# The first gated block's transposition, by squares and DRAM in place of TensorE, inside the output projection

## The chip, the cores and the metric

The kernel runs on one core of a Trainium2 chip. The metric is the time of one execution on the device in microseconds (us), the median of several runs; lower is better. One execution was also recorded by the hardware profiler. TensorE does the matmuls, VectorE (DVE in the profile) and ScalarE (ACT) the elementwise work and the copies out of the accumulators, GpSimd (POOL) small work and some transfers, and SyncE (SP) issues most transfers. ScalarE can issue transfers too.

## The reference

Two layers, each an attention block and a gated block, with a residual and a layer norm ahead of each. There are 2048 tokens of width 448, 16 heads of width 28, and a hidden width of 1792.

```python
def _A_ref(x, wqkv, wo):                      # attention
    qkv = (x @ wqkv).reshape(B, S, 3, H, Dh).transpose(2, 0, 3, 1, 4)
    q, k, v = qkv[0], qkv[1], qkv[2]
    p = _softmax(jnp.einsum("bhqd,bhkd->bhqk", q, k) * (Dh ** -0.5))
    o = jnp.einsum("bhqk,bhkd->bhqd", p, v)
    return o.transpose(0, 2, 1, 3).reshape(B, S, D) @ wo
def _B_ref(x, w_gate, w_up, w_down):          # gated block
    h = _sigmoid(x @ w_gate) * (x @ w_up)
    return h @ w_down
x = A_x
for layer in range(2):                        # written out in the reference
    x = x + _A_ref(_layernorm(x), A_wqkv, A_wo)
    x = x + _B_ref(_layernorm(x), B_w_gate, B_w_up, B_w_down)
```

## The kernel before

The residual `x` stays in SBUF as 16 tiles of 128 tokens by 448 features. Four tiles make a block of 512 tokens (`TB` = 4, `NB` = 4). Operands of matmuls are pairs of float16 numbers, a high part and a low part, so one exact product costs several matmuls.

The order of instructions on every engine is that in which the program emits them. There is no scheduler (`manual_schedule`); semaphores are set between engines where tiles depend on each other. An instruction that waits holds everything behind it on its engine, and a transfer that waits holds everything behind it on its queue.

A layer has four stages: `project` (queries, keys, values), `attend`, `out_project` and `gated`. This case is about the seam between the last two.

`out_project` multiplies the 16 token tiles with the output weights, 11 matmuls of 448 columns for each tile: nine for the feature groups 0 to 2 (lines 517 to 519), two for the tail (lines 514 and 515), which holds the last head. Six tiles are done early without their tails (`early` = 6), since the last head's rows come late by transfers; then the six tails, then the other ten tiles. After each tile VectorE adds the result onto `x` (`add`, line 1199).

The gated block works on a `Block` of 512 tokens: layer norm (`stats`, `scale`), transposition to features by tokens, and a list of seven steps, `half_steps`, which builds the operands of a product scheme by halves: `r11`, `t1`, `t2`, `t3` make the four parts of `wide`, and `r21`, `t4`, `r22` make the three parts of `short`. Every step makes one high part by a copy on ScalarE (`divide`), one low part by a subtraction on VectorE, and mostly a difference on VectorE (`subtract`). The last three also copy a part from 64 lower partitions to the upper ones on ScalarE (`double`, line 376).

There are two ways to transpose. TensorE does it with an identity matrix, 16 transposes a block (`turn`, line 443), and ScalarE copies the result out of the accumulators (`turn_raw`, line 455). Or VectorE transposes squares of 32 by 32 (`squares`, line 295), the result is written to DRAM (`store`, line 307), and read back with rows and columns of squares in place (`gather`, line 315). With the second way the tokens lie in an order of squares, and a step that reads the gathered tile does so in two operations of half the size, where the first way takes one (the `cut`, `subtract` and `divide` of `half_steps`). The later blocks of `gated` use the second way; the first block, made inside `out_project`, uses the first.

`gated` emits, for each block and each pair of weight columns `p`, the products of `gate_and_up` on TensorE, in this order: `first(0)`, `first(1)`, `apart(0)`, `second(0)`, `second(1)` and so on. `first(0)` and `second(0)` are written to the same accumulator bank (`chain[0]`); between them ScalarE copies the bank out (line 1319). The products need `wide` for the first seven and `short` after that. Weights come in parts: `gu(p)` for gate and up, `dn` for down. `out_project` issues the loads of `gu(1)`, one `dn` and `gu(2)` on SyncE's queue at its start, and `gated` issues more at its own.

Of the kernel before, what the change touches and what calls it, by code (L numbers as in the profile page):

```python
# [16 lines left out]
ALU = mybir.AluOpType  # L17
AX = mybir.AxisListType

P = 128  # L20
S = 2048
D = 448
# [5 lines left out]
TB = NT // NB  # L28
W = TB * P
NF = F // P  # L30
NQ = D // 32
# [74 lines left out]
def interleaved_layers(ctx: ExitStack, tc: tile.TileContext, x_in, wqkv, wo, w_gate, w_up,  # L106
                       w_down, out):
    nc = tc.nc
# [6 lines left out]
    big = Slots(spool, "s", N_SLOTS)  # L115
# [5 lines left out]
    def new_banks():  # L121

        if banks["stack"] is not None:
            banks["stack"].close()
        uid[0] += 1
        banks["stack"] = ExitStack()
        banks["pool"] = banks["stack"].enter_context(
            tc.tile_pool(name=f"psum{uid[0]}", bufs=1, space=bass.MemoryType.PSUM,
                         reuse_waits="tile"))

    def psum(tag, name, shape):
        uid[0] += 1
        return banks["pool"].tile(shape, F32, name=f"{name}_{uid[0]}", tag=tag, bufs=1)
# [4 lines left out]
    def bank(i, name):  # L138
        return psum(f"bank{i}", name, [P, 512])
# [105 lines left out]
    class Block:  # L245
# [10 lines left out]
        def __init__(self, b, halves=False):  # L256
            self.b = b
            self.halves = halves
            self.turned = False

        def norm(self, js=range(TB)):
            b = self.b
# [77 lines left out]
        def half_steps(self):  # L340
            def cut(k, t):

                if self.turned:
                    return self.raw[:, k:k + 2, t * P:(t + 2) * P]
                return self.raw[:, k:k + 2, :].rearrange(
                    "p k (i t c) -> p k t i c", i=4, t=TB)[:, :, t:t + 2]

            def ordered(v):
                return v.rearrange("p k (t i c) -> p k t i c", t=2, i=4)

            def subtract(name, a, b):
                t = qrt.get(name, [P, 2, W // 2])
                if self.turned:
                    nc.vector.tensor_tensor(t, a, b, op=ALU.subtract)
                    return t
                a, b = [v if len(v.shape) == 5 else ordered(v) for v in (a, b)]
                for k in range(2):
                    nc.vector.tensor_tensor(ordered(t)[:, k], a[:, k], b[:, k],
                                            op=ALU.subtract)
                return t  # L360

            def divide(to, v):

                hi, lo = to[:, 0], to[:, 1]
                if len(v.shape) == 5:
                    for k in range(2):
                        nc.scalar.copy(ordered(hi)[:, k], v[:, k])
                        nc.vector.tensor_tensor(ordered(lo)[:, k], v[:, k], ordered(hi)[:, k],
                                                op=ALU.subtract)
                else:  # L370
                    nc.scalar.copy(hi, v)
                    nc.vector.tensor_tensor(lo, v, hi, op=ALU.subtract)

            def double(to):

                nc.scalar.copy(to[64:P, 0, 1], to[0:64, 0, 1])

            def r11():
                self.wide = big.get("xwide", [P, 4, 2, 2, W // 2], F16)
                self.short = big.get("xshort", [P, 3, 2, 2, W // 2], F16)  # L380
                self.t1 = subtract("t1", cut(0, 2), cut(0, 0))
                divide(self.wide[:, 0], cut(0, 0))

            def t1():
                self.t2 = subtract("t2", cut(2, 2), self.t1)
                divide(self.wide[:, 1], self.t1)
                qrt.put(self.t1)

            def t2():
                self.t3 = subtract("t3", cut(2, 2), cut(0, 2))  # L390
                divide(self.wide[:, 2], self.t2)

            def t3():
                self.t4 = subtract("t4", cut(2, 0), self.t2)
                nc.gpsimd.memset(self.t4[64:P, 1, :], 0.0)
                divide(self.wide[:, 3], self.t3)
                qrt.put(self.t2, self.t3)

            def r21():
                divide(self.short[:, 0], cut(2, 0))  # L400
                double(self.short[:, 0])

            def t4():
                divide(self.short[:, 1], self.t4)
                double(self.short[:, 1])
                qrt.put(self.t4)

            def r22():
                divide(self.short[:, 2], cut(2, 2))
                double(self.short[:, 2])  # L410
                big.put(self.raw)

            return [r11, t1, t2, t3, r21, t4, r22]

        def ready(self, *kts):
            if kts[0] == 0:
                self.parts()
            for kt in kts:
                self.part(kt)


        def begin(self):
            uid[0] += 1
            self.mv = cpool.tile([P, TB, 2], F32, name=f"mv_{uid[0]}", tag="mv", bufs=2)
            self.rs = cpool.tile([P, TB], F32, name=f"rs_{uid[0]}", tag="rs", bufs=2)
            self.xn = big.get("xn", [P, TB, D])
# [13 lines left out]
        def turn(self, j):  # L440
            for kt in self.pt:
                c = slice(kt * P, min((kt + 1) * P, D))
                nc.tensor.transpose(self.pt[kt][0:c.stop - c.start, j * P:(j + 1) * P],
                                    self.xn[:, j, c], ident)

        def turn_raw(self):
            self.turned = True
            self.turn_banks(4, range(4))
            self.raw = big.get("xraw", [P, 4, W])
            nc.gpsimd.memset(self.raw[64:P, 3, :], 0.0)  # L450
            for j in range(TB):
                self.turn(j)
            for kt, pt in self.pt.items():
                n = P if kt < 3 else 64
                nc.scalar.copy(self.raw[0:n, kt, :], pt[0:n])
            big.put(self.xn)

        def turned_high(self):
            for kt, pt in self.pt.items():
# [50 lines left out]
    def by_tokens(pm, hi, lo, tail, w, kts=range(4)):  # L510

        for kt in kts:
            if kt == 3:
                nc.tensor.matmul(pm, tail, w[:, 0, 3, :], start=False, stop=False)  # L514
                nc.tensor.matmul(pm, tail, w[:, 1, 3, :], start=False, stop=True)  # L515
                continue
            nc.tensor.matmul(pm, hi(kt), w[:, 0, kt, :], start=(kt == 0), stop=False)  # L517
            nc.tensor.matmul(pm, hi(kt), w[:, 1, kt, :], start=False, stop=False)  # L518
            nc.tensor.matmul(pm, lo(kt), w[:, 0, kt, :], start=False, stop=False)  # L519
# [88 lines left out]
    def run_fill(fill, n=1):  # L608
        for _ in range(n):
            if fill:  # L610
                fill.popleft()()
# [574 lines left out]
    def out_project(outs, gate):  # L1186
        new_banks()
        nc.scalar.activation(warm, warm, AF.Sigmoid)
        nc.scalar.reg_load(gate_scale, back.bitcast(I32)[0:1, 3:4])
        first = Block(0, True)  # L1190
        steps = deque([first.turn_raw] + first.half_steps())
        early = 6

        def products(pm, t, kts):
            by_tokens(pm, outs.hi(t), outs.lo(t), outs.tail(t) if 3 in kts else None, gate.out,
                      kts)

        def add(pm, t):
            nc.vector.scalar_tensor_tensor(x[:, t, :], pm, back[:, 1:2], x[:, t, :],
                                           op0=ALU.mult, op1=ALU.add)  # L1200

        gate.load_gu(1)
        gate.load_dn()
        gate.load_gu(2)
        pms = [bank(t, "op")[:, 0:D] for t in range(early)]
        for t in range(early):
            products(pms[t], t, range(3))
        first.begin()
        for t in range(early):
            products(pms[t], t, [3])  # L1210
            add(pms[t], t)
            if t < TB:
                first.stats(t)
            if t >= TB:
                first.scale(t - TB)
        for j in range(early - TB, TB):
            first.scale(j)
        for t in range(early, NT):
            pm = bank(t if t < 8 else t % 4, "op")[:, 0:D]
            products(pm, t, range(4))  # L1220
            add(pm, t)
            if t >= 9:
                run_fill(steps, 2 if t == 9 else 1)
        big.put(*outs.kt, gate.out)
        run_fill(steps, 9)
        return first
# [181 lines left out]
    first = Block(0)  # L1408
# [29 lines left out]
    for layer in range(LAYERS):  # L1438
        values, heads, last_values = project(layer, wq, first)
        gate = WeightsGated()  # L1440
        outs = attend(layer, values, heads, last_values, gate, wq.keep)
        mlp_first = out_project(outs, gate)
        wq = WeightsQKV()

        def before_next(f, wq=wq):
            if f == 6:
                wq.load()

        first = gated(layer, mlp_first, gate, before_next)
# [28 lines left out]
```

## Time and profile before

| | |
|---|---|
| time, median of 3 runs | 1940.18 us (1938.45 to 1941.05) |
| the profiled execution's own time | 1939.73 us |
| its span | 1937.9 us |
| granted TensorE clock, mean | 0.997 |
| TensorE busy | 1919.4 us, 99% of the span |
| VectorE busy | 1234.5 us, 64% |
| ScalarE busy | 1316.6 us, 68% |

A row of the timeline has the start in the span, the duration, the engine, the line, the operation with its output and inputs, the shapes and the count of instructions merged in it. In square brackets stand the idle time of the engine ahead of it and what ended that. The matmuls' durations overlap; the distance of two starts is what one costs. A row of the windows gives the busy time of each engine in a stretch, the granted TensorE clock as a share of full speed, the DMA engines' busy share and GB/s. A row of DMA issues has the size of each.

### The profile page before, as it was taken

The numbers are of one execution on the slowest core, as the hardware profiler recorded it, in microseconds if no ns is written. First come the engines' busy times: TensorE is split into PE (matmuls) and PEld (weight loads), VectorE is DVE, ScalarE is ACT, GpSimd is POOL, SyncE is SP. The second block draws the span as 40 slices with busy tenths as digits, with TensorE's granted clock in tenths as the row PEclk, the third lists the DMA queues.
The fourth block names the chain that finished last, engine by engine and source line by source line (L and its number), as shares of the span: only waits on it lengthen the run. The fifth ranks groups of instructions, "written<-read, shape, count | busy, mean of one in ns | idle before, by whom it ended". The sixth has DMA issues, their size and how long they took to land. (4 is left out here: it accounts for less than half of the span.)

```text
span 1937.9 us, 53581 instructions
## 1 busy us (share of the span) xinstructions
PE 1919.4 (99%) x23405; PEld 1321.1 (68%) x23405; DVE 1234.5 (64%) x2325; ACT 1316.6 (68%) x1577; POOL 165.4 (9%) x307
## 2 busy tenths in 40 slices
PE   9999999999999999999999999999999999999999
PEld 4445555556556777777744577778898777777776
DVE  7628878788655555555375477787778664655543
ACT  5559999999993343444345799999999644343432
POOL 2013322211001000000000000000000000000000
PEclk9999999999999999999999999999999999999999
DMA  5565664334216313232244321122111243333310
GB/s 171 163 203 152 185 201 127 116 89 125 64 61 241 107 69 107 75 134 78 87 125 126 98 51 32 45 50 51 36 41 65 95 176 118 107 107 97 117 50 20
DMA packets 90518, 201.53 MB, mean 104 GB/s; under 512 B 10814, under 2 KB 58014, under 8 KB 90144
## 3 DMA queue, kind: packets, MB, share of 16 engines
q1 hardware_dynamic: 65664, 111.02, 19.3%
q0 software_dynamic: 17776, 83.51, 12.9%
q8 instruction: 188, 3.08, 0.7%
q10 hardware_dynamic: 6832, 3.44, 0.7%
q14 instruction: 58, 0.48, 0.1%
HBM read 142.61 MB, written 47.98 MB: 98 GB/s over the span
## 5 line engine op out<-in xcount | busy, mean ns | idle before, releaser
L1046 ACT ACTIVATE prob_s<-sc 128x1536 f32<-128x1536 f32 x659 | 891.4, 1491 | 6.2 <-PE sc L1031 5.7
L1082 PE MATMUL acc<-prob_s,val_s 128*32 128x256 f32 (+3 forms) x7748 | 589.3, 383 | 0.0
L1031 PE MATMUL sc<-qp_s 114*32 114x512 f16 x7896 | 575.6, 380 | 4.4 <-issue 2.2
L507 PEld LDWEIGHTS <-gu_s 128*128 128x128 f16 x4368 | 427.3, 98 | 60.9 <-issue 1.7
L1031 PEld LDWEIGHTS <-qp_s 114*32 114x32 f16 x8192 | 310.6, 96 | 181.0 <-issue 80.2
L1082 PEld LDWEIGHTS acc<-prob_s,val_s 128*32 128x32 f32 x7748 | 316.0, 110 | 100.7 <-issue 6.9
L1335 DVE TENSOR_TENSOR one_q<-side,one_q 128x512 f32<-128x512 f32 x112 | 72.0, 684 | 305.8 <-PE side L507 305.6
L507 PE MATMUL chain<-xwide_s,gu_s 128*128 128x256 f16 x2016 | 247.5, 273 | 0.6 <-ACT one_q L1319 0.5
L1319 ACT COPY one_q<-chain 128x256 f32<-128x256 f32 x224 | 83.0, 373 | 205.4 <-PE chain L507 201.6
L1062 DVE SCALAR_TENSOR_TENSOR power_q<-power_q,expo_q 128x512 f32<-128x512 f32 x222 | 153.6, 692 | 7.6
L1289 PE MATMUL dnp<-dn_s,hhl_q 128*128 128x448 f16 x448 | 157.9, 352 | 0.0
L1290 PE MATMUL dnp<-dn_s,hhl_q 128*128 128x448 f16 x448 | 157.9, 352 | 0.0
L1288 PE MATMUL dnp<-dn_s,hhl_q 128*128 128x448 f16 x448 | 157.9, 352 | 0.0
L507 PE MATMUL side<-xshort_s,gu_s 128*128 128x256 f16 x1120 | 140.9, 272 | 0.3 <-DVE one_q L1335 0.3
L492 PE MATMUL qkp<-xhl_s,wqk_s 128*128 128x512 f16 x616 | 138.0, 379 | 2.2 <-DVE xhl_s L206 0.7
L1111 DVE STREAM_TRANSPOSE oturned_q<-acc 128x512 f32<-128x512 f32 x32 | 22.9, 716 | 142.5 <-PE acc L1082 142.5
L492 PEld LDWEIGHTS <-wqk_s 128*128 128x128 f16 x616 | 60.3, 98 | 72.2 <-issue 2.8
L1056 DVE TENSOR_SCALAR expo_q<-aside,base 128x512 f32<-128x512 f32 x74 | 55.4, 748 | 58.1 <-PE aside L1031 57.8
L507 PE MATMUL side<-xwide_s,gu_s 128*128 128x256 f16 x672 | 91.7, 273 | 0.0
L1319 ACT COPY two_q<-chain 128x256 f32<-128x256 f32 x112 | 41.7, 373 | 67.4 <-PE chain L507 67.4
L1082 PE MATMUL acc<-power_q,val_s 128*32 128x128 f32 (+3 forms) x276 | 86.4, 394 | 0.0
L1346 ACT ACTIVATE one_q<-one_q 128x512 f32<-128x512 f32 x56 | 35.3, 630 | 59.8 <-DVE one_q L1335 59.8
(185 smaller groups left out, 2078.8 us busy)
## 6 DMA issues: line engine op xcount, KB each, us to landing
gu_s<-gu_parts POOLq DMA_DIRECT2D x56, 800.0 KB, 4.8
qp_s<-qk_scr SPq DMA_DIRECT2D x96, 224.0 KB
gu_s<-gu_parts SPq DMA_DIRECT2D x20, 800.0 KB
qk_scr<-qkhl_q SPq DMA_DIRECT2D x56, 256.0 KB
gu_parts<-pack_s POOLq DMA_DIRECT2D x14, 800.0 KB, 3.9
xraw_s<-xt_scr SPq DMA_DIRECT2D x12, 768.0 KB
xt_scr<-xs_s SPq DMA_DIRECT2D x34, 224.0 KB
qp_s<-qk_scr SPq DMA_DIRECT2D x64, 112.0 KB
```

The source lines that it names most:

```text
L492: nc.tensor.matmul(pm, w, x, start=(i == 0), stop=(i == len(terms) - 1))
L507: nc.tensor.matmul(pm, a, x, start=(first and i == 0), stop=(i == len(terms) - 1), skip_group_check=True)
L1031: nc.tensor.matmul(ps[32 * j:32 * j + 32, :], hd.k[:, keys], hd.q[:, qb * W:(qb + 1) * W], start=True, stop=True, tile_position=(0, 32 * j))
L1046: nc.scalar.activation(prob[:, 0:n, :], ps[:, 0:n, :], AF.Exp, scale=exp_scale)
L1056: nc.vector.tensor_scalar(y, ps, base2[:, 0:1], -126.0, op0=ALU.mult, op1=ALU.max)
L1062: nc.vector.scalar_tensor_tensor(p, p, c[k], y, op0=ALU.add, op1=ALU.mult)
L1082: nc.tensor.matmul(acc[qb * VC:(qb + 1) * VC, s], v[:, kc % TB, h, :], probs[c * NB + qb][:, s], start=(kc == 0 and a == 0), stop=(kc == N ...
L1288: nc.tensor.matmul(pm, hl[:, 0, s], dw[:, 0, :], start=begin, stop=False)
L1289: nc.tensor.matmul(pm, hl[:, 0, s], dw[:, 1, :], start=False, stop=False)
L1290: nc.tensor.matmul(pm, hl[:, 1, s], dw[:, 0, :], start=False, stop=end)
L1319: nc.scalar.copy(to, pm)
L1335: nc.vector.tensor_tensor(one[m], side[m], one[m], op=ALU.add)
```

## The change

In `out_project` the first gated block is transposed by squares and DRAM. Four tiles are early in place of six. Each of the four gets its add, its statistics and, one tile later, its scaling and its 32x32 transposes, all on VectorE ahead of the other tiles' adds. Then the two stores on SyncE's queue and two on ScalarE's are issued, and the gather; the loads of `dn` and `gu(2)` come after the gather on SyncE's queue. The seven steps start at tile 12, one with each tile, and the last three follow tile 15; before, TensorE's transposes and `r11` came with tile 9, and the others with tiles 10 to 15. The accumulator banks of the 16 tiles are numbered by `(t + 4) % 8`.

```diff
+        def square(self, j):
+
+            if j == 0:
+                self.xs = big.get("xs", [P, NQ, TB, 32])
+            self.scale(j)
+            nc.vector.transpose(self.xs[:, :, j, :], self.xn[:, j, :])
+            if j == TB - 1:
+                big.put(self.xn)
...
-        def turn_raw(self):
-            self.turned = True
-            self.turn_banks(4, range(4))
-            self.raw = big.get("xraw", [P, 4, W])
-            nc.gpsimd.memset(self.raw[64:P, 3, :], 0.0)
-            for j in range(TB):
-                self.turn(j)
-            for kt, pt in self.pt.items():
-                n = P if kt < 3 else 64
-                nc.scalar.copy(self.raw[0:n, kt, :], pt[0:n])
-            big.put(self.xn)
...
         first = Block(0, True)
-        steps = deque([first.turn_raw] + first.half_steps())
-        early = 6
+        steps = deque(first.half_steps())
+        early = 4
...
         gate.load_gu(1)
-        gate.load_dn()
-        gate.load_gu(2)
-        pms = [bank(t, "op")[:, 0:D] for t in range(early)]
+        pms = [bank((t + 4) % 8, "op")[:, 0:D] for t in range(early)]
         for t in range(early):
             products(pms[t], t, range(3))
         first.begin()
         for t in range(early):
             products(pms[t], t, [3])
             add(pms[t], t)
-            if t < TB:
-                first.stats(t)
-            if t >= TB:
-                first.scale(t - TB)
-        for j in range(early - TB, TB):
-            first.scale(j)
+            first.stats(t)
+            if t:
+                first.square(t - 1)
+        first.square(TB - 1)
+        first.store((nc.sync, nc.scalar))
+        first.gather()
+        gate.load_dn()
+        gate.load_gu(2)
         for t in range(early, NT):
-            pm = bank(t if t < 8 else t % 4, "op")[:, 0:D]
+            pm = bank((t + 4) % 8, "op")[:, 0:D]
             products(pm, t, range(4))
             add(pm, t)
-            if t >= 9:
-                run_fill(steps, 2 if t == 9 else 1)
+            if t >= 12:
+                run_fill(steps)
         big.put(*outs.kt, gate.out)
         run_fill(steps, 9)
         return first
```

With `turned` gone, the two short branches in `half_steps` that read the gathered tile whole are gone too.

More of the change, by code (lines that the diff above doesn't have):

```diff
@@ L258, in __init__ @@
             self.halves = halves
-            self.turned = False
         def norm(self, js=range(TB)):
@@ L341, in cut @@
             def cut(k, t):
-                if self.turned:
-                    return self.raw[:, k:k + 2, t * P:(t + 2) * P]
                 return self.raw[:, k:k + 2, :].rearrange(
@@ L352, in subtract @@
                 t = qrt.get(name, [P, 2, W // 2])
-                if self.turned:
-                    nc.vector.tensor_tensor(t, a, b, op=ALU.subtract)
-                    return t
                 a, b = [v if len(v.shape) == 5 else ordered(v) for v in (a, b)]
```

## The prediction

> **What bounds the kernel now.** I read the page's busy shares first, then TensorE's timeline through the first layer's output projection, then VectorE's and ScalarE's through the same stretch. All times are microseconds from the start of the span, in the first layer unless said.
>
> ```profile
> PE 1919.4 (99%) x23405; PEld 1321.1 (68%) x23405; DVE 1234.5 (64%) x2325; ACT 1316.6 (68%) x1577; POOL 165.4 (9%) x307
> ```
>
> TensorE is busy 99% of the span, the others at most 68%. So a TensorE instruction that goes saves its time, and a TensorE wait that comes costs its time, unless later idle absorbs it; and with 1% idle there is none to absorb. TensorE's timeline of the projection and of the first gated products behind it:
>
> ```profile
> 577.96 0.36 PE L517 MATMUL op<-wout_s,ot_s 128*128 128x448 f16 x1
> ...
> 588.18 0.35 PE L514 MATMUL op<-wout_s,ot_s 128*128 128x448 f16 x1
> 588.37 0.35 PE L515 MATMUL op<-wout_s,ot_s 128*128 128x448 f16 x1
> ...
> 598.78 1.91 PE L443 MATMUL turn<-ident,xn_s 128*128 128x128 f32 x16
> 600.52 0.35 PE L517 MATMUL op<-wout_s,ot_s 128*128 128x448 f16 x1
> ...
> 613.01 1.47 PE L507 MATMUL chain<-xwide_s,gu_s 128*128 128x256 f16 x12
> 614.32 0.82 PE L507 MATMUL side<-xwide_s,gu_s 128*128 128x256 f16 x6
> 615.38 1.47 PE L507 MATMUL chain<-xwide_s,gu_s 128*128 128x256 f16 x12 [0.24 <-ACT one_q L1319]
> ```
>
> The 54 matmuls of six tiles from 577.96 to 588.18 give a pitch of 10.22/54 = 0.189. The 16 transposes take 600.52 - 598.78 = 1.74. With 176 matmuls: 577.96 + 33.31 + 1.74 = 613.01, the row of the first gated product, so the projection runs without a gap. What matters is the last row: the third gated product (the second use of the chain's bank) waits 0.24 for ScalarE's copy of the first. ScalarE was late there already. Its timeline says why:
>
> ```profile
> 610.37 0.40 ACT L376 COPY xshort_s<-xshort_s 64x256 f16<-64x256 f16 x1 [2.48 <-DVE xshort_s L372]
> 610.79 0.62 ACT L371 CAST xshort_s<-t_q 128x512 f16<-128x512 f32 x1
> 612.45 0.40 ACT L376 COPY xshort_s<-xshort_s 64x256 f16<-64x256 f16 x1 [1.04 <-DVE xshort_s L372]
> 612.86 0.62 ACT L371 CAST xshort_s<-xraw_s 128x512 f16<-128x512 f32 x1
> 614.53 0.40 ACT L376 COPY xshort_s<-xshort_s 64x256 f16<-64x256 f16 x1 [1.05 <-DVE xshort_s L372]
> 614.95 0.65 ACT L1319 COPY one_q<-chain 128x256 f32<-128x256 f32 x2
> ```
>
> ScalarE works in program order: the copy of the first gated product (L1319) stands behind the last doubling (L376) of the step `r22`, and starts at 614.95, 0.02 after it ends, though its product began at 613.01. So the real bound at this seam is when the seven steps `r11` to `r22` are done, not TensorE.
>
> **What the change takes away.** Sixteen transposes in each layer: 1.74 of TensorE, all on the path, and four copies of ScalarE, which lay beside other work. TensorE's first gated product comes at 577.96 + 176 x 0.189 = 611.28. The four early tiles need the last head's rows after 36 matmuls (584.77) in place of 54 (588.18); I price that wait at nothing, but it isn't in the trace; each 0.1 of it would add 0.1.
>
> **What it adds on VectorE early.** Four 32x32 transposes, and the order add, statistics, scale, transpose for tiles 0 to 3.
>
> ```profile
> 588.76 0.68 DVE L1199 SCALAR_TENSOR_TENSOR x<-op,back,x 128x448 f32<-128x448 f32 x1 [6.98 <-PE op L515]
> ...
> 590.24 0.65 DVE L1199 SCALAR_TENSOR_TENSOR x<-op,back,x 128x448 f32<-128x448 f32 x1
> ...
> 640.97 0.47 DVE L278 TENSOR_SCALAR xn_s<-x,mv,rs 128x448 f32<-128x448 f32 x1
> 641.48 0.65 DVE L295 STREAM_TRANSPOSE xs_s<-xn_s 128x448 f32<-128x448 f32 x1
> ```
>
> An add starts 0.39 after the start of its tile's last matmul (588.76 against 588.37). The first is then at 577.96 + 37 x 0.189 + 0.39 = 585.35. Each tile costs 1.48 for add and statistics and some 1.1 for scale and transpose; four tiles end near 585.35 + 4 x 2.6 = 595.7. TensorE isn't held by that: tile 8 is the first to take a bank again, after 88 matmuls (594.6), and needs only tile 0's add.
>
> **The round trip through DRAM.** Two stores on SyncE's queue and two on ScalarE's start at 595.7, the gather follows. The nearest rows:
>
> ```profile
> 1028.53 3.52 SPq L307 DMA_DIRECT2D xt_scr<-xs_s  x4
> 1035.32 0.38 SPq L315 DMA_DIRECT2D xraw_s<-xt_scr  x1
> ...
> 1040.05 1.14 ACT L200 CAST xhl_s<-xraw_s 128x512 f16<-128x512 f32 x2 [0.29 <-DMA xraw_s<-xt_scr]
> ...
> 1691.41 0.84 ACTq L307 DMA_DIRECT2D xt_scr<-xs_s  x2
> 1696.38 0.38 SPq L315 DMA_DIRECT2D xraw_s<-xt_scr  x1
> ...
> 1000.12 0.39 SPq L315 DMA_DIRECT2D xraw_s<-xt_scr  x1
> 1005.71 1.66 ACT L200 CAST xhl_s<-xraw_s 128x512 f16<-128x512 f32 x3 [3.76 <-DMA xraw_s<-xt_scr]
> ```
>
> From the store's issue to the gather's: 4.97 (two on ScalarE's queue, SyncE's two long issued) to 6.79 (four on one queue). From the gather's issue to the first reader: 4.73 to 5.59. So the data is in use between 605.4 and 608.1; I take 606.7, near the middle, because the four stores run at once as in neither row. Behind the gather SyncE's queue now holds the loads of `dn` and `gu(2)` that were issued at the start of the projection, and those that `gated` issues. Their sizes, the rate of such loads (last column of the window's row, GB/s) and their first use:
>
> ```profile
> gu_s<-gu_parts SPq DMA_DIRECT2D x20, 800.0 KB
> ...
> dn_s<-dn_parts SPq DMA_DIRECT2D x6, 896.0 KB
> ...
> 603.00:604.00 1.00, 1.00 (x7) 0.54 (x6) 0.97 (x2) 0.52 (x1) 0.00 (x0) 1.00 1.02 418
> ...
> 630.65 0.35 PE L1288 MATMUL dnp<-dn_s,hhl_q 128*128 128x448 f16 x1
> ```
>
> One part of `dn` and the two of `gu(2)` are 2496 KB, 6 us at 418 GB/s, so landed by about 613; the first use (`dn`, 630.65) is 17 away. Cost nothing; without that cover it would be the part by which they pass 630.
>
> **The seven steps, moved to the end.** This is the term that decides. They began at tile 9 and now begin at tile 12, one behind each tile's add; `r21`, `t4` and `r22`, which lay in the shade of tiles 13 to 15, now run after tile 15. The pieces:
>
> ```profile
> 606.63 0.69 DVE L372 TENSOR_TENSOR xwide_s<-t_q,xwide_s 128x512 f16<-128x512 f32 x1
> 607.23 0.68 DVE L1199 SCALAR_TENSOR_TENSOR x<-op,back,x 128x448 f32<-128x448 f32 x1
> ...
> 609.65 0.68 DVE L372 TENSOR_TENSOR xshort_s<-xraw_s,xshort_s 128x512 f16<-128x512 f32 x1
> ...
> 658.71 0.71 ACT L367 CAST xwide_s<-xraw_s 128x256 f16<-128x256 f32 x2
> 659.44 0.75 DVE L358 TENSOR_TENSOR t_q<-xraw_s 128x256 f32<-128x256 f32 x2
> 660.11 0.75 DVE L368 TENSOR_TENSOR xwide_s<-xraw_s,xwide_s 128x256 f16<-128x256 f32 x2
> ```
>
> On VectorE an add or a whole 128x512 operation takes 0.60 to the next start (606.63 to 607.23); a pair of halves, into which the gathered layout cuts every operation on `raw`, takes 0.67 (659.44 to 660.11). Tile 15's last matmul starts at 577.96 + 175 x 0.189 = 611.09, its add at 611.48; then `t4` by halves 612.08, the low part of `t3` 612.75, the pair of `r21` 613.35, ending 0.75 later at 614.10. From there the two engines alternate, each waiting for the other. A hand-over takes 0.02 to 0.04 (the low part of 609.65 ends at 610.33, the doubling starts at 610.37 and ends at 610.77, the cast starts at 610.79). Doubling 0.40, cast of `t4` 0.62, its low part 0.68, doubling 0.40, first cast of `r22` 0.40, its pair of low parts 0.75, doubling 0.40 make 3.65, and eight hand-overs of 0.03 make it 3.89. ScalarE's copy of the first gated product starts at 617.99 where it was 614.95. TensorE's third product started 0.43 behind that, at 615.38, so it is at 618.42 now: **+3.04 in each layer**, the 1.74 saved already counted. TensorE stands idle from 611.28 + (615.14 - 613.01) = 613.41 to 618.42, 5.0. VectorE's steps `r11` to `t3` with the adds between take 2 x 0.67 + 3 x 1.87 = 6.95 before `r21`, so data in use after 613.35 - 6.95 = 606.4 delays all this one for one: with 606.7, **+0.3** (0 to 1.7).
>
> **The clock behind that idle.** The trace has one place in the middle of the work where the granted clock fell, before the first scores (in the windows' rows: length, TensorE busy, granted clock, DMA share, GB/s):
>
> ```profile
> 125.18 2.32 PE L1031 MATMUL sc<-qp_s 114*32 114x512 f16 x18 [1.99 <-issue]
> 124.00:126.00 2.00, 0.82 (x9) 0.68 0.99 284
> 126.00:128.00 2.00, 2.00 (x16) 0.50 1.04 241
> ```
>
> After a gap of 1.99 the granted clock was 0.68 and 0.50 in two stretches of 2: (2 x 0.32 + 2 x 0.50)/0.5 = 3.3 at half speed, which costs 1.6 of work. A gap of 5.0 must do at least that; part of the half-speed time can fall into the idle itself (then some 0.8), or it can last twice as long (up to 2.5). I take **+1.5** (0 to 2.5). The Trainium skill, "TensorE: Matmul & The Clock Gate", Part 1, says that the clock is halved after a whole idle window of about 3.4 us, that the windows run freely, and that a busy window restores it. By that rule an idle of 5.0 would hold a whole window in (5.0 - 3.4)/3.4, about half of the cases, and the sum would be 4.9 a layer in these and 3.3 in the others. The trace agrees with the length (3.3) and not with the condition: no gap there was longer than the 1.99 of the row, and the clock fell.
>
> **The sum.** 3.04 + 0.3 + 1.5 = 4.84 a layer. The second layer has the same seam (one row: the same copy is waited for, 0.24):
>
> ```profile
> 1569.22 1.47 PE L507 MATMUL chain<-xwide_s,gu_s 128*128 128x256 f16 x12 [0.24 <-ACT one_q L1319]
> ```
>
> So 9.7 on the profiled execution's 1939.73, **1949.4**. That execution lies 0.45 (0.02%) under the median of 1940.18, which I neglect.
>
> **Rivals.** (1) The clock stays: the idle is 5 us, but no half-speed time follows. 2 x 3.34 on 1939.73 = 1946.4. For it: the drop shows at one place only, and there two stretches with few matmuls followed each other (0.82 busy of 2.00). Against: that row of 0.50 stands behind a gap of less than half the length. Chance 0.17; by the skill's rule it would be about 0.5. (2) The gather is late: the four stores slow each other and the data is in use at 608.1 or later; 1.7 in place of 0.3, so 1952.2. For it: the 6.79, and loads queued behind the gather on the same queue. Against: the loads that filled the queues in the row of 603.00 now come behind it, so the stores have them to themselves. Chance 0.15. (3) **The other side, faster**: ScalarE's copy isn't late, because the steps end before TensorE needs the bank again. The transposes' 1.74 and the old wait's 0.24 are saved, 3.96 in both layers, 1935.8. The point of decision is the copy's start: before 614.95 the change gains, after it loses. For it: VectorE has free time between 598 and 605 and the steps are short. Against: they stand behind the add of tile 12 in program order, at 577.96 + 142 x 0.189 + 0.39 = 605.2, so that time is no use to them, and 12 us of alternation follow. Chance 0.08. My forecast has the remaining 0.60.
>
> **How the numbers follow.** No change means within 0.2% of 1940.18 (3.9 us, about what a measurement of this kernel can tell): 1936.3 to 1944.1. Rival 3 lies at that edge, so I split it: 0.04 faster, 0.04 same; 0.01 more for same from rival 1 at its lowest. The rest, 0.91, is slower. With the bounds of the gather and the clock a layer costs 3.04 to 3.04 + 1.7 + 2.5, so 1945.8 to 1954.2; both ends need everything on one side, and the hand-overs are uncertain by a few tenths. The range is 1944.5 to 1953.5, which holds rivals 1 and 2 at their likely times and leaves out rival 3 and the worst of rival 2, together under 0.2.
>
> **What would show it.** Right: no transposes in the projection, the first gated product 33.3 after the projection's first matmul, then TensorE idle for about 5 "for ACT one_q L1319" in each layer, and the granted clock at 0.5 for some 3 behind it; ScalarE's copy right behind a doubling. The gather step would show in VectorE's wait before `r11`. Wrong: if that wait is under 1, or if the third product waits for something other than ScalarE's copy, say a weight that is still on its way.

## The result and the profile after

The changed kernel takes 1951.98 us, median of six runs (1949.97 to 1953.88), against 1939.59 for the kernel before (1938.45 to 1941.05, six runs). The ratio is 1.0063, with a 95% interval of 1.0053 to 1.0073: slower, as predicted, by 0.6%, and inside the range, 2.6 us above the predicted time. The profiled execution took 1951.14 with a span of 1949.4, so 11.5 more than the span before.

TensorE does less and takes longer. The page's first lines:

```profile
span 1949.4 us, 53527 instructions
...
PE 1918.5 (98%) x23373; PEld 1256.8 (64%) x23373; DVE 1241.4 (64%) x2347; ACT 1312.8 (67%) x1575; POOL 165.7 (9%) x307
```

There are 32 TensorE instructions fewer (the transposes of two layers), and the idle has grown from 18.5 us to 30.9. In the list of TensorE's waits one entry, which was 0.5 us in all before, has grown to 13.1, and it covers that growth (in total, times, longest):

```profile
PE chain L498 <- ACT one_q L1310: 13.1, 2, 6.6
```

TensorE's timeline of the first layer's seam, and the same product in the second layer. The line numbers are nine lower than before: 498 is the product that was 507, 1310 the copy that was 1319.

```profile
577.05 0.36 PE L508 MATMUL op<-wout_s,ot_s 128*128 128x448 f16 x1
...
610.36 1.47 PE L498 MATMUL chain<-xwide_s,gu_s 128*128 128x256 f16 x12
611.67 0.82 PE L498 MATMUL side<-xwide_s,gu_s 128*128 128x256 f16 x6
619.12 2.72 PE L498 MATMUL chain<-xwide_s,gu_s 128*128 128x256 f16 x12 [6.63 <-ACT one_q L1310]
...
985.61 0.35 PE L1281 MATMUL dnp<-dn_s,hhl_q 128*128 128x448 f16 x1
...
1578.56 2.72 PE L498 MATMUL chain<-xwide_s,gu_s 128*128 128x256 f16 x12 [6.44 <-ACT one_q L1310]
```

The first gated product comes 33.31 after the projection's first matmul (35.05 before). The third waits 6.63 and starts 42.07 after the projection's first matmul (37.42 before). It then takes 2.72 where the first took 1.47: the clock. The row of 985.61 is the gated stage's last matmul, 408.56 after the projection's first. In the kernel before, the row of that matmul gives 401.74:

```profile
979.69 0.35 PE L1290 MATMUL dnp<-dn_s,hhl_q 128*128 128x448 f16 x1
```

So the two stages together cost 6.82 more in layer 1, and 6.36 more in layer 2 by the same rows there: 13.18 in all.

ScalarE's timeline shows what the third product waited for:

```profile
614.83 0.40 ACT L370 COPY xshort_s<-xshort_s 64x256 f16<-64x256 f16 x1 [1.91 <-DVE xshort_s L362]
615.25 0.62 ACT L365 CAST xshort_s<-t_q 128x512 f16<-128x512 f32 x1
616.63 0.40 ACT L370 COPY xshort_s<-xshort_s 64x256 f16<-64x256 f16 x1 [0.76 <-DVE xshort_s L366]
617.04 0.71 ACT L361 CAST xshort_s<-xraw_s 128x256 f16<-128x256 f32 x2
618.27 0.40 ACT L370 COPY xshort_s<-xshort_s 64x256 f16<-64x256 f16 x1 [0.52 <-DVE xshort_s L362]
618.70 0.65 ACT L1310 COPY one_q<-chain 128x256 f32<-128x256 f32 x2
```

The copy of the first gated product stands right behind the last doubling, as before, but 41.65 after the projection's first matmul where it was 37.0. Each step ahead of it waits for VectorE's half of it. The product itself had been done since 611.8 (610.36 and the 1.47 of its row).

Where the steps' own start comes from, by VectorE's and SyncE's timelines:

```profile
584.46 0.69 DVE L1190 SCALAR_TENSOR_TENSOR x<-op,back,x 128x448 f32<-128x448 f32 x1 [3.60 <-PE op L506]
...
594.45 0.65 DVE L420 STREAM_TRANSPOSE xs_s<-xn_s 128x448 f32<-128x448 f32 x1
...
607.09 0.76 DVE L352 TENSOR_TENSOR t_q<-xraw_s 128x256 f32<-128x256 f32 x2 [2.09 <-DMA xraw_s<-xt_scr]
```

```profile
595.13 0.86 SPq L306 DMA_DIRECT2D xt_scr<-xs_s  x2
601.63 0.39 SPq L314 DMA_DIRECT2D xraw_s<-xt_scr  x1
```

Stores issued at 18.08 after the projection's first matmul, the gather 6.50 later, its data in use 5.46 after that, at 30.04. VectorE waited 2.09 for it.

The granted clock behind the idle, by windows (length, busy time of TensorE, its weight loads, VectorE, ScalarE and GpSimd, granted clock, DMA share, GB/s):

```profile
616.00:617.00 1.00, 0.00 (x0) 0.00 (x0) 0.59 (x1) 0.37 (x1) 0.00 (x0) 0.94 1.02 417
617.00:619.00 2.00, 0.00 (x0) 0.00 (x0) 0.76 (x2) 1.44 (x6) 0.00 (x0) 0.50 1.05 434
619.00:623.00 4.00, 3.88 (x19) 2.68 (x19) 0.00 (x0) 1.09 (x4) 0.00 (x0) 0.50 1.01 415
623.00:624.00 1.00, 1.00 (x8) 0.74 (x7) 0.00 (x0) 0.00 (x0) 0.00 (x0) 0.65 1.03 423
```

The 0.94 puts the start of half speed at 616.9, the 0.65 its end at 623.7: 6.8 in all, of which 4.6 lie behind the third product's start and cost half, 2.3.

### The profile page after: what moved, and what is told of

The parts are those of the page before. It is cut to its first block, busy times and chain, and to the rows that moved or that the text cites. A ratio compares the mean times of both kernels' runs of the same rounds, so it can differ in the third digit from the quotient of the medians.

```text
span 1949.4 us, 53527 instructions
## 1 busy us (share of the span) xinstructions
PE 1918.5 (98%) x23373; PEld 1256.8 (64%) x23373; DVE 1241.4 (64%) x2347; ACT 1312.8 (67%) x1575; POOL 165.7 (9%) x307
## 5 line engine op out<-in xcount | busy, mean ns | idle before, releaser
L1073 PE MATMUL acc<-prob_s,val_s 128*32 128x256 f32 (+3 forms) x7748 | 573.5, 383 | 0.0
L1022 PE MATMUL sc<-qp_s 114*32 114x512 f16 x7896 | 558.0, 379 | 3.2 <-issue 1.7
L1022 PEld LDWEIGHTS <-qp_s 114*32 114x32 f16 x8192 | 277.0, 95 | 207.4 <-issue 94.1
L1073 PEld LDWEIGHTS acc<-prob_s,val_s 128*32 128x32 f32 x7748 | 281.2, 110 | 135.2 <-issue 11.4
L498 PE MATMUL chain<-xwide_s,gu_s 128*128 128x256 f16 x2016 | 250.6, 275 | 13.2 <-ACT one_q L1310 13.1
```

Of the source, the lines that this page charges most:

```text
L498: nc.tensor.matmul(pm, a, x, start=(first and i == 0), stop=(i == len(terms) - 1), skip_group_check=True)
L1022: nc.tensor.matmul(ps[32 * j:32 * j + 32, :], hd.k[:, keys], hd.q[:, qb * W:(qb + 1) * W], start=True, stop=True, tile_position=(0, 32 * j))
L1073: nc.tensor.matmul(acc[qb * VC:(qb + 1) * VC, s], v[:, kc % TB, h, :], probs[c * NB + qb][:, s], start=(kc == 0 and a == 0), stop=(kc == N ...
```

## The experiments

The theory: the copy is late because the last steps stand ahead of it in ScalarE's program order; the wait starts the half-speed stretch, which costs more; and the round trip adds what its data comes late. The rivals: the price lies in the DRAM round trip itself, or in the loads behind it, or the clock's drop costs nothing in the end.

All times first. "Two stages" is the distance from the projection's first matmul to the gated stage's last, in both layers of the profiled execution, against 803.59 before. "Rest" is the span without these stages, in which all kernels run the same code. Each ratio is to executions of the kernel before that were taken beside the run (medians 1938.77 to 1939.77).

| kernel | time, us (runs) | ratio to before, 95% interval | two stages | rest |
|---|---|---|---|---|
| before | 1939.59 (6) | | 803.59 | 1134.3 |
| after | 1951.98 (6) | 1.0053 to 1.0073 | +13.18 | 1132.6 |
| after, again | 1954.20 (5) | 1.0062 to 1.0088 | +13.42 | 1136.8 |
| e1, TensorE kept busy | 1950.96 (4) | 1.0043 to 1.0076 | +8.44 | 1137.5 |
| e1, again | 1950.83 (5) | 1.0043 to 1.0069 | +8.78 | 1136.7 |
| e2, before with late steps | 1951.37 (4) | 1.0049 to 1.0082 | +12.72 | 1132.0 |
| e3, steps behind the copies | 1939.94 (10) | 0.9996 to 1.0015 | +1.21 | 1137.2 |
| e4, steps together | 1936.46 (10) | 0.9976 to 0.9995 | -4.13 | 1135.3 |
| e4, again | 1937.06 (11) | 0.9976 to 0.9994 | -4.08 | 1135.0 |
| e5, loads later | 1951.73 (6) | 1.0052 to 1.0079 | +11.75 | 1135.7 |
| e6, stores twice | 1960.59 (4) | 1.0095 to 1.0129 | +22.13 | 1131.9 |
| e7, one queue | 1951.33 (4) | 1.0039 to 1.0073 | +12.98 | 1135.6 |

The rest lies between 1131.9 and 1137.5, and for the one kernel after at 1132.6 and 1136.8. So single executions differ by some 4 us for reasons outside the change, while the two stages of one kernel repeat within 0.4. What is finer than 4 us is read from the stages first, and from the medians second. One of these reasons shows in the traces: TensorE's clock also falls to half, for 3.4 us at a time, at places outside the two stages, and not in every execution. One such place lies before the first scores. Its window in the first execution of after, where the clock stayed, and of e1, where it fell:

```profile
126.00:128.00 2.00, 1.97 (x23) 0.89 (x23) 0.00 (x0) 1.33 (x1) 0.00 (x0) 1.00 1.07 251
```

```profile
126.00:128.00 2.00, 2.00 (x11) 0.62 (x6) 0.00 (x0) 2.00 (x2) 0.00 (x0) 0.50 1.04 225
```

After's first execution, e2, e4's second and e6 have no such stretch in the rest, apart from the start and the end of the span (1131.9 to 1135.0), e3 has two, and the others have one (1134.3 to 1137.5). A stretch of 3.4 at half speed is 1.7 of lost work, so it accounts for a part of the 4 us; what makes up the remainder is open.

**e2: the steps alone.** The kernel before, with TensorE's transposes and without DRAM, and only the seven steps moved to where the change has them.

```diff
-            if t >= 9:
-                run_fill(steps, 2 if t == 9 else 1)
+            if t == 9 or t >= 12:
+                run_fill(steps)
```

> The kernel before with one part of the change alone: TensorE's transposes stay at tile 9, the loads stay early, six early tiles, no squares and no DRAM, but the seven steps start at tile 12, one behind each tile. Theory (where the steps stand in program order is the cost): r21, t4 and r22 run behind tile 15, ScalarE's copy of the first gated product starts about 41.8 behind the projection's first matmul in place of 37.0, 4.8 us later, and the idle halves the clock, some 2 more: 6.8 a layer, 1953 (1950 to 1956). Rival (the round trip through DRAM and the loads behind it are the cost): 1939.6, as before.

1951.37, ratio 1.0066. TensorE's timeline and ScalarE's:

```profile
618.36 2.47 PE L507 MATMUL chain<-xwide_s,gu_s 128*128 128x256 f16 x12 [5.04 <-ACT one_q L1319]
```

```profile
617.50 0.40 ACT L376 COPY xshort_s<-xshort_s 64x256 f16<-64x256 f16 x1 [0.76 <-DVE xshort_s L372]
617.93 0.65 ACT L1319 COPY one_q<-chain 128x256 f32<-128x256 f32 x2
```

Without any round trip the same copy stands behind the same doubling, the wait is 5.04 and the time is the changed kernel's. The place of the steps is enough for a loss of this size. That the two times agree is in part chance. The third product comes 4.80 later here, which is the prediction's 3.04 and the 1.74 of the transposes that this kernel keeps (4.78). The changed kernel saves the 1.74, and loses 1.6 in layer 1 by late data.

**e3: the order alone.** The changed kernel with the round trip and all else, but the last three steps are emitted behind the first copies of the gated products in place of ahead of them.

```diff
-        run_fill(steps, 9)
+        first.rest = steps
         return first
...
             first(0)
             first(1)
             apart(0)
+            run_fill(rest)
             second(0)
             second(1)
             apart(1)
+            run_fill(rest)
             third(0)
             third(1)
+            run_fill(rest)
```

> The changed kernel with r21, t4 and r22 emitted inside the first gate_and_up: r21 behind apart(0), t4 behind apart(1), r22 behind third(1), so that ScalarE's copies of the first two products stand ahead of them. Nothing else changes; the data comes from DRAM as late. Theory: no single wait of TensorE over 2 us, the clock stays, the first c12 begins some 43 us behind the projection's first matmul, as in the kernel before (42.9): 1940.5 (1939 to 1942.5). Rival (the data's lateness itself is the cost, whatever stands behind it): 1948 or more.

1939.94, no different from before. ScalarE, then TensorE:

```profile
613.42 0.62 ACT L365 CAST xwide_s<-t_q 128x512 f16<-128x512 f32 x1 [1.25 <-DVE t_q L352]
613.94 0.64 ACT L1310 COPY one_q<-chain 128x256 f32<-128x256 f32 x2
```

```profile
612.07 1.47 PE L498 MATMUL chain<-xwide_s,gu_s 128*128 128x256 f16 x12
...
614.36 1.47 PE L498 MATMUL chain<-xwide_s,gu_s 128*128 128x256 f16 x12 [0.17 <-ACT one_q L1310]
...
617.41 1.47 PE L498 MATMUL chain<-xwide_s,gu_s 128*128 128x256 f16 x12 [0.92 <-ACT two_q L1310]
```

The wait of 6.63 is 0.17, and no product runs longer than 1.47: a reorder of three steps gives back 12.0 of the 13.2 in the two stages. What is left are small waits at the next copies (0.92 in the last row), each again behind a step. This kernel still has the round trip, with its data in use at 30.07. So the round trip alone doesn't make the loss: with it, 1.2 of the 13.2 are left. Its late data costs what it does in the changed kernel (1.6 and 1.4 a layer, and a longer half-speed stretch) because the steps that wait for it stand ahead of the copy.

**e1: the clock alone.** The changed kernel with 27 products that nobody reads in TensorE's idle of the seam.

```diff
             apart(0)
+            for i in range(busy):          # busy = 27 for b == 0 and p == 0, else 0
+                if i == 0:
+                    spare = bank(0, "spare")
+                nc.tensor.matmul(spare, w[0][:, 0], w[0][:, 0:4], start=(i == 0),
+                                 stop=(i == busy - 1))
             second(0)
```

> The changed kernel with 27 extra matmuls of 512 columns (5.8 us at full speed) behind the first gate_and_up's apart(0) in each layer, into a bank that nothing else uses then; their result is not used. TensorE's wait for ScalarE's copy stays as long, but TensorE is busy in it. Theory (order on ScalarE, plus the halved clock behind the idle): the granted clock stays at 1.0 behind the seam, and the 4.6 and 4.3 us of half speed that lie behind the idle in the changed kernel cost nothing, so 2.3 + 2.1 = 4.4 us less than the changed kernel's 1952.0: 1947.6 (1946.5 to 1948.7). The copy of the first gated product starts as late as in the changed kernel, 41.6 behind the projection's first matmul. Rival (the half-speed stretch is hidden by other engines): 1952.

> The 27 idle-time products once more, beside the kernel after on the same chip. If the clock's drop costs what the seams show, the time is 4.4 to 4.7 us below the kernel after of this call (1947.5 where that is 1952; ratio about 1.004), and the seams are 8.4 us longer than before instead of 13.2. The rival, that the clock's drop is paid back elsewhere (a later stage gives the gain away again): the seams are shorter and the time is the same as after's within 1 us.

TensorE's timeline of the second run:

```profile
611.68 5.99 PE L1348 MATMUL spare<-gu_s 128*128 128x512 f16 x27
618.25 1.47 PE L498 MATMUL chain<-xwide_s,gu_s 128*128 128x256 f16 x12 [0.57 <-ACT one_q L1310]
```

The product behind the copy takes 1.47 again, and the copy is as late as in the changed kernel (41.41 against 41.44 after the projection's first matmul in after's second run). The two stages are 4.74 shorter than after's in the first runs of both kernels and 4.64 in the second. In the first runs 0.48 of this isn't the clock's: the third product of e1 starts 0.32 and 0.16 sooner than after's, as its data came sooner. In the second runs these products start 0.08 later in sum. So the clock's price, measured by taking it away, is 2.1 a layer by the first runs and 2.4 by the second. In time the first run was a miss: 1950.96, 1.0 below after where 1947.6 was expected, with a rest of 1137.5 against 1132.6. Of these 4.9, some 1.7 are the stretch of half speed before the first scores that only e1's execution has. Taken beside the kernel after on the same chip it was 1950.83 against 1954.20, 3.4 less where 4.4 to 4.7 were expected, and the spans differ by 4.7. That the gain is given back by a later stage doesn't hold: what differs between the two pairs is the rest, and after's own rest moves as much.

This was expected of the second run of the kernel after, taken beside the second run of e1:

> The kernel after, once more, as the measure for the others of this call: 1952 us (1950 to 1954), ratio about 1.0063. Projection and gated stage together about 13.2 us longer than before over both layers, of it 4.4 by TensorE at half speed behind the two idles; two half-speed stretches of 6.8 us, one at each seam.

Its time came out 2.2 above the first run's and just over the expected upper end; its two stages are within 0.3 of the first's.

**e6 and e7: what sets the time of the stores.** The prediction took a middle value for the round trip, which came late. e6 issues each store of the first block twice, once into a copy that nobody reads; e7 puts all four on SyncE's queue.

```diff
             for i in range(4):
                 r = slice(32 * i, 32 * i + 32)
+                queues[i % len(queues)].dma_start(
+                    copy[:, :, i, :].rearrange("j r n -> r j n"),
+                    xs[r].rearrange("r j t c -> r j (t c)"))
                 queues[i % len(queues)].dma_start(
                     self.scr[:, :, i, :].rearrange("j r n -> r j n"),
                     xs[r].rearrange("r j t c -> r j (t c)"))
```

```diff
-        first.store((nc.sync, nc.scalar))
+        first.store((nc.sync,))
```

> The kernel after, with each of the first block's four stores issued twice, once into a copy that nobody reads, ahead of the store proper on the same queue. Twice 4 x 224 KB then lie ahead of the gather. If the stores' own transfer sets the 6.5 us from store to gather (the DMA engines were 0.91 to 0.96 busy there at 176 to 206 GB/s), 896 KB more at 190 GB/s add 4.7 us: 11.2 from store to gather, data in use at 34.7 behind the projection's first matmul, the third product 4.7 later in each layer, time 9 to 10 us above the kernel after (1961). The rival, that most of the 6.5 is a fixed latency of a transfer: from store to gather 7.5 at most, time at most 2 us above after.

> The kernel after, with the four stores all on SyncE's queue instead of two on SyncE's and two on ScalarE's. If the DMA engines are what the stores wait for, one queue keeps them as busy as two and 6.5 us from store to gather stays (6.4 to 6.9), data in use at about 30.0 to 30.3, time as after's within 1 us. The rival, that each queue carries its own stores one behind the other: from store to gather over 8, the third product 2 us later in each layer, time 4 us above after's.

e6 took 1960.59. Its timelines of SyncE and of VectorE, then the windows while the stores run, first of e6 and then of the changed kernel:

```profile
594.47 0.33 SPq L310 DMA_DIRECT2D xt_copy<-xs_s  x1
...
606.16 0.39 SPq L321 DMA_DIRECT2D xraw_s<-xt_scr  x1
```

```profile
611.04 0.76 DVE L359 TENSOR_TENSOR t_q<-xraw_s 128x256 f32<-128x256 f32 x2 [6.70 <-DMA xraw_s<-xt_scr]
```

```profile
596.00:604.00 8.00, 8.00 (x44) 4.11 (x42) 3.77 (x7) 0.00 (x0) 0.00 (x0) 1.00 0.93 185
```

```profile
596.00:600.00 4.00, 4.00 (x23) 2.08 (x22) 2.71 (x5) 0.00 (x0) 0.00 (x0) 1.00 0.93 191
```

From store to gather it is 11.69 where it was 6.50, and the third product comes 4.60 later in layer 1 and 4.40 in layer 2. The DMA engines are 0.93 busy at 185 and 191 GB/s, for 8 us in place of 4. So most of the 6.5 is the stores' own transfer: 896 KB at 191 GB/s are some 4.8 of it, and 896 KB more added 5.19. e7 says the same from the other side; all four on one queue:

```profile
596.20 3.02 SPq L306 DMA_DIRECT2D xt_scr<-xs_s  x4
602.66 0.39 SPq L314 DMA_DIRECT2D xraw_s<-xt_scr  x1
```

6.46 from the first store to the gather, 6.50 with two queues; 1951.33 us. Here it makes no difference whether the stores stand on one queue or on two.

**e5: the loads behind the gather.** The changed kernel with the loads of `dn`, of `gu(2)` and of the gated stage's first weights on GpSimd's queue, emitted after the tiles, so that they are issued from 616 on, when the gather has long landed.

```diff
         first.gather()
-        gate.load_dn()
-        gate.load_gu(2)
         for t in range(early, NT):
             ...
+        gate.load_dn(nc.gpsimd)
+        gate.load_gu(2, nc.gpsimd)
...
-        wt.load_dn()
-        wt.load_gu(3)
+        wt.load_dn(nc.gpsimd)
+        wt.load_gu(3, nc.gpsimd)
...
```

> The kernel after, with the loads of dn, of gu(2) and of the gated stage's first weights issued on GpSimd's queue behind the first block's rounding, so that no transfer is issued behind the gather until it has landed. If those loads slow the gather, it lands 0.4 to 0.8 us sooner after its issue (4.7 to 5.0 instead of 5.46), the third product follows as much sooner in each layer, and the time is about 1 us below the kernel after. The rival, that the late landing is the four stores' own time and the gather's own latency: data in use still 30.0 behind the projection's first matmul, and the time as after's within 1 us.

The gather and its first reader, in layer 1 and in layer 2:

```profile
603.50 0.39 SPq L314 DMA_DIRECT2D xraw_s<-xt_scr  x1
...
1564.27 0.39 SPq L314 DMA_DIRECT2D xraw_s<-xt_scr  x1
```

```profile
609.10 0.76 DVE L352 TENSOR_TENSOR t_q<-xraw_s 128x256 f32<-128x256 f32 x2 [2.24 <-DMA xraw_s<-xt_scr]
...
1569.15 0.76 DVE L352 TENSOR_TENSOR t_q<-xraw_s 128x256 f32<-128x256 f32 x2 [1.41 <-DMA xraw_s<-xt_scr]
```

5.60 in one layer and 4.88 in the other, against 5.46 and 5.48 in after's first run and 5.25 and 5.20 in its second. Layer 1 went against the theory, layer 2 with it. In e6, with the loads back behind the gather, it was 4.88 and 4.72. So the loads aren't shown to slow the gather, and the leg moves between 4.7 and 5.6 for a reason that stays open. In time e5 is 2.5 below after's second run, beside which it was taken, and 0.3 below after's first. Its two stages are 1.4 to 1.7 shorter than after's, nearly all of it in layer 2: there the data came sooner, TensorE idled 5.95 in place of 6.44, and the half speed lasted 3.4 in place of 6.8 (granted clock 0.78 in 1580 to 1581, 0.50 up to 1583, 0.52 up to 1584, then 1.00).

**e4: a version that gains.** The changed kernel with `r11`, `t1`, `t2`, `t3` and all reads of the gathered tile put together at tile 12, so that VectorE and ScalarE work side by side in place of by turns. What is left (the cast of `t4`, three doublings, the adds of tiles 13 to 15) stands behind the copies.

```diff
+            if apart:
+                r11()
+                t1()
+                high(self.short[:, 0], cut(2, 0))
+                t2()
+                high(self.short[:, 2], cut(2, 2))
+                t3()
+                low(self.short[:, 0], cut(2, 0))
+                low(self.short[:, 2], cut(2, 2))
+                big.put(self.raw)
+                return [last, lambda: double(self.short[:, 1]), lambda: double(self.short[:, 2])]
...
-            add(pm, t)
-            if t >= 12:
-                run_fill(steps)
+            if t <= 12:
+                add(pm, t)
+            if t == 12:
+                first.rest = first.operands()
+            if t > 12:
+                first.rest.append(lambda pm=pm, t=t: add(pm, t))
...
             apart(0)
+            run_fill(rest)
             second(0)
             second(1)
             apart(1)
+            run_fill(rest, 5)
```

> The changed kernel with all of VectorE's and ScalarE's work on the gathered tile together at tile 12 (the adds of tiles 13 to 15 behind it, ScalarE's casts of raw as soon as it has time), and the three doublings, with the cast of t4, behind ScalarE's first two copies in the first gate_and_up. Theory: no wait of TensorE for ScalarE is left at the seam, so the 1.74 of the transposes and the 0.24 of the old wait are saved in each layer: 1935.7 (1935 to 1938), faster than the kernel before by 0.2%. Rival (data in use at 30.0 behind the projection's first matmul is too late for any order): 1941 or more, with TensorE waiting for xwide or xshort.

> The version with tile 12's steps put together and the rest behind the first copies, once more with five rounds: 4 us below before (ratio 0.9979, 0.997 to 0.999), as its seams are 4.1 us shorter over both layers. The rival: that 4 us of the seams is within what the other stages vary by, and the ratio's interval holds 1.

1936.46 and 1937.06, ratios 0.9986 and 0.9985, both intervals below 1: faster than the kernel before by about 0.14%, and than the changed one. TensorE's timeline of the first run has no wait at the seam:

```profile
610.50 1.47 PE L526 MATMUL chain<-xwide_s,gu_s 128*128 128x256 f16 x12
...
612.47 1.47 PE L526 MATMUL chain<-xwide_s,gu_s 128*128 128x256 f16 x12
```

The third product comes 35.27 after the projection's first matmul, 2.15 sooner than before: the transposes' 1.74, the old wait of 0.24, and a little more. The two stages are 4.1 shorter in both runs. In time 2.3 us of it arrive, by the medians against the kernel before taken beside it; the expected 4 lies inside both intervals.

## Why the prediction was right, and what it had too small

The kernel is slower for the reason given: the seven steps at tile 12, and ScalarE's copy behind them. e2 shows it without the round trip and e3 by taking it away. By the prediction's own steps:

- **What the change takes away** held. The first gated product came at 33.31 (predicted 33.3). The early tails made no one wait: the first add starts 7.41 after the projection's first matmul, predicted 7.39.
- **VectorE's early work** ended 0.34 later than predicted: the stores were issued at 18.08 after the projection's first matmul, not 17.74.
- **The round trip is the step that failed.** Predicted 11.0 from store to use, measured 11.96 in layer 1. With the 0.34 of the line above, the data is in use at 608.0 on the prediction's axis, not 606.7. The break-even of 606.4 was right: the third product came 4.65 late, which is the predicted 3.04 and the 1.6 by which the data passed 606.4 (4.45 and 1.4 in layer 2). The prediction put +0.3. It took a middle between 4.97 and 6.79 for the stores. But the 4.97 counted from two stores while two others were long issued, whereas here all four, 896 KB, had to pass, at the 185 to 191 GB/s of e6 and after. The row of four stores on one queue, 6.79, was the right one, though by that row it seemed to belong to one queue only; e7 shows that the queue makes no difference. Against rival 2 the prediction held that the stores would have the queues to themselves; they did, and alone they kept the DMA engines 0.93 busy. Of the 0.96, some 0.6 lie between store and gather (6.50, where the middle of the bounds was 5.88) and 0.3 behind the gather (5.46, where the middle was 5.16); the cause of the second part is open.
- **The seven steps** held, piece by piece. From the data's use to the pair of `r21` it is 6.95 (predicted 6.95), and from there to the third product 5.08 (predicted 5.07).
- **The clock** was too small: +1.5 predicted, 2.2 and 1.9 measured (6.82 less 4.65, 6.36 less 4.45), 2.1 to 2.4 by e1. The idle was 6.63, not 5.0, because of the late data, and half speed lasted 6.8, not 3.3. In e2, with 5.04 as predicted, it cost 1.65 (6.45 more in the two stages of layer 1, 4.80 of it from the late product). So most of this miss follows from the one before.
- **The loads behind the gather** cost nothing: from the last gated product of the first pair of weight columns to the first down product it is 9.82, as before.
- **The sum**: 6.8 and 6.4 a layer, not 4.84 (which the paragraph on the clock gives as 4.9). Of the 3.5 missing over both layers, 2.4 are the late data (0.7 of it by the later start of the stores, the rest the round trip's) and 1.1 the clock.
- **The rivals.** The clock's staying (1) falls. The late gather (2) is nearly what came: the data in use at 608.0 for its 608.1, and its 1952.2 is the measured time; its reason, that the stores slow each other, is what e6 shows. It deserved more than 0.15. The faster side (3) falls for the reason given against it, and e3 and e4 show that its point of decision, the copy's start, was the right one.

The Trainium skill, "TensorE: Matmul & The Clock Gate", Part 1, asks for a whole idle window of about 3.4 us before the clock is halved. The seams agree: half speed behind idles of 6.63, 6.44 and 5.04, none behind e1's 0.57 or e3's 0.92; the gap of 1.99 in the kernel before remains against it. So does layer 2 of e3, where the clock fell behind gaps of 1.89 and 0.35:

```profile
1009.25 0.38 PE L483 MATMUL qkp<-xhl_s,wqk_s 128*128 128x512 f16 x1 [1.89 <-ACT xhl_s L200]
```

```profile
1011.00:1014.00 3.00, 3.00 (x9) 1.01 (x7) 1.47 (x4) 1.02 (x3) 0.00 (x0) 0.50 0.18 45
```

## What to carry to other kernels

Where work moves to the end of a stage, look on every engine at the next stage's first instruction behind it: an engine that works in order makes that one wait for all of it, and three steps on the wrong side of one copy cost 12 us here, over two layers. Price a group of transfers by the row in which as many bytes lie ahead of the reader (here 6.79, measured 6.50), not by the landing of those that were issued last; their bytes over the rate that the windows show, 4.8 here, are only the least of it. And a wait of 5 us or more on TensorE cost more than its length in all twelve seams that had one: another 1.2 to 2.6 at half speed, taken as the growth of the two stages less the third product's delay.

## What the runs showed of the hardware

The half-speed stretch grew with the idle ahead of it, in steps of about 3.4. It was 6.8 behind the seven idles of 6.26 to 6.78 (after twice, e7, layer 1 of e5), and 3.4 behind the 5.95 of e5's layer 2 and the 5.04 of e2, by these windows of e2 (from 618.66 to 622.06 by the same reckoning as above):

```profile
618.00:619.00 1.00, 0.65 (x5) 0.53 (x5) 0.00 (x0) 0.58 (x2) 0.00 (x0) 0.83 0.99 403
619.00:622.00 3.00, 3.00 (x16) 2.13 (x15) 0.00 (x0) 0.74 (x2) 0.00 (x0) 0.50 0.47 196
622.00:623.00 1.00, 1.00 (x11) 0.86 (x10) 0.00 (x0) 0.16 (x1) 0.00 (x0) 0.97 0.00 0
```

In e6 the third product waited longer still, and the windows show 10.2:

```profile
PE chain L505 <- ACT one_q L1317: 15.9, 2, 8.0
```

```profile
617.00:618.00 1.00, 0.00 (x0) 0.00 (x0) 1.00 (x4) 0.00 (x0) 0.31 (x1) 0.91 0.96 401
618.00:628.00 10.00, 4.93 (x24) 3.41 (x24) 2.19 (x6) 3.93 (x10) 1.28 (x2) 0.50 1.02 419
628.00:629.00 1.00, 1.00 (x11) 0.88 (x10) 0.00 (x0) 0.41 (x2) 0.00 (x0) 0.97 1.01 416
```

The stores of the transposed squares, in runs of 128 float32 numbers, kept the DMA engines 0.93 busy at 185 to 191 GB/s, where the weights' loads in the rows above move 415 to 434 GB/s at a share of about 1: about half as much for the same busy time. Whether the short runs are the reason wasn't tested.
